# Decode attention over a long K/V cache: late MLP weights, eight stream buffers instead of six, and V before K on the tensor engine

## The chip, the cores and the metric

The kernel runs on one core of a Trainium2 chip. Times are device microseconds of one execution. The profiler's span, from the first to the last instruction, is 1.8 us shorter than the reported time (before: 702.1 of 703.9 us). Step times below are on the span's clock.

Engine names: PE is the tensor engine (PEld its weight loads), DVE the vector engine, ACT the scalar engine, POOL and SP the two others. SP issues nearly all loads.

## The reference, cut to what matters

One token passes through one block: layer norm, attention of 32 query heads over 8 K/V heads with 65,536 cached positions of 128 values each, output projection, residual, layer norm, a gated MLP with 1,792 hidden values, residual. All tensors are bf16.

```python
h  = x + (softmax(q @ k.T * Dh**-0.5) @ v) @ wo          # q = layernorm(x) @ wq
h2 = h + (sigmoid(hn @ w_gate) * (hn @ w_up)) @ w_down    # hn = layernorm(h)
```

K and V are 268 MB, the weights 14 MB; everything is read once, so the kernel is a stream of 282 MB through the core.

## The kernel before

K and V arrive as 128 tiles of 2 MB (128 partitions, 64 positions of 128 values in each). A K tile is transposed on PE, copied from PSUM by DVE and ACT, and multiplied with q ("S2"). A V tile is multiplied with the exponentials ("PV"). K of head h is interleaved with V of head h-1. SP issues the load of tile `ti` when tile `ti - NB` has been used up. The gate, up and down weights (5.5 MB) ride between early tiles. Cuts are marked.

```python
NB = 6
kvbuf = [sb(f"kvbuf{i}", [P, NSL, DH], BF) for i in range(NB)]
wg_sb = sb("wg_sb", [P, DC, F], BF); wu_sb = ...; wd_sb = ...
pexp = [sb(f"pexp{i}", [P, REP, CH], BF) for i in range(2)]
# ... wchunks: four pieces of wo on s_wo, then gate, up and two halves of down on s_wglu ...

def process_k_tile(h, t, b, vt, kti):
    pe.wait(s_buf[b], 16 * fill_count[b])
    # ... 64 transposes, evacuations, S2 groups three behind ...
    if vt is not None:
        pv_emit_all(vt)              # the V tile that came before this K tile

for ti, (kind, h, t) in enumerate(tiles):
    run_deferred(ti)
    b = ti % NB
    if ti - NB >= 0:
        sp.wait(ch_tile.sem, rel[ti - NB])
    # ... the last tile as four loads s_last[0..3] ...
    sp.dma(lambda e: e.dma_start(kvbuf[b][:, :, :], src_t), s_buf[b])
    wi = ti - (NB - 1)
    if 0 <= wi < len(wchunks):       # one weight piece after each of tiles 5 to 12
        sp.dma(wchunks[wi] ...)
    # ... process the tile ...

# the tail, after the last PV: softmax sum, o, output projection, layer norm, then
pe.wait(s_wglu, 16 * N_WGLU_DMA)
# ... 112 gate and up matmuls in two halves, tanh, product, 2 x 28 down matmuls, output ...
```

Of the kernel before, what the change touches and what calls it, by code (L numbers as in the profile page):

```python
# [5 lines left out]
BF = mybir.dt.bfloat16  # L6
F32 = mybir.dt.float32
ACTF = mybir.ActivationFunctionType
ALU = mybir.AluOpType
# [90 lines left out]
def bass_sequential_preLN__gqa_block_cached__glu_gated_glu__decode_kernel(  # L100
# [28 lines left out]
    FILL = min(128, CH)  # L129
    assert CH % FILL == 0 and FILL % GS == 0  # L130
    FPH = CH // FILL
    NB = 6
    NS = 5
    LAG = 3
    SCALE = float(DH) ** -0.5
# [24 lines left out]
    with ExitStack() as es:  # L160
# [6 lines left out]
        wbig = sb("wbig", [P, WBIG], BF)  # L167
        wq_v = wbig[:, 0:DC * HQ * DH].rearrange("p (c n) -> p c n", c=DC)
        wo_v = wbig[:, 0:HQ * D].rearrange("p (hd n) -> p hd n", hd=HQ)
        wg_sb = sb("wg_sb", [P, DC, F], BF)  # L170
        wu_sb = sb("wu_sb", [P, DC, F], BF)
        wd_sb = sb("wd_sb", [P, FC, D], BF)
        sc = [sb(f"sc{i}", [P, REP, CH], F32) for i in range(2)]
        pexp = [sb(f"pexp{i}", [P, REP, CH], BF) for i in range(2)]
        ident_f = sb("ident_f", [P, P], F32)
        ident_b = sb("ident_b", [P, P], BF)
        ones_f = sb("ones_f", [P, P], F32)
        onesD_f = sb("onesD_f", [P, P], F32)
        eps_t = sb("eps_t", [P, 1], F32)
        xcol_b = sb("xcol_b", [P, DC], BF)  # L180
        xx = sb("xx", [P, 2 * DC], F32)
        hh = sb("hh", [P, 2 * DC], F32)
        stat = sb("stat", [P, 8], F32)
# [10 lines left out]
        rs4 = sb("rs4", [P, 1], F32)  # L194
        o4_b = sb("o4_b", [P, P], BF)
        o_b = sb("o_b", [P, HQ], BF)
        attn_acc = sb("attn_acc", [P, DC], F32)
        th = sb("th", [P, FC], F32)
        sig = sb("sig", [P, FC], F32)
        hid_b = sb("hid_b", [P, FC], BF)  # L200
# [20 lines left out]
        s_wbig = sem("s_wbig")  # L221
        s_wo = sem("s_wo")
        s_x = sem("s_x")
        s_wglu = sem("s_wglu")
        s_out = sem("s_out")
        NQ_LAST = 4
        s_last = [sem(f"s_last{i}") for i in range(NQ_LAST)]
# [19 lines left out]
        def W(stream, inc):  # L247
# [17 lines left out]
            ),  # L265
            g_ident,
        )
        for c in range(DC):
            act.dma(
                lambda e, c=c: e.dma_start(  # L270
                    xcol_b[:, c:c + 1],
                    A_x[0, 0, c * P:(c + 1) * P].rearrange("(p o) -> p o", o=1),
                ),
                s_x,
            )

        def issue_wglu(stream):
# [11 lines left out]
            )  # L289

        sp.dma(
            lambda e: e.dma_start(wq_v, A_wq.rearrange("(c p) n -> p c n", p=P)),
            s_wbig,
        )

# [6 lines left out]
        W(dve, g_ident)  # L302
        d_identb = ch_dm.nxt()
        dve.ins(lambda e: e.tensor_copy(ident_b[:, :], ident_f[:, :]), d_identb)
        dve.wait(s_x, 16 * DC)
        d1 = ch_dm.nxt()
        dve.ins(lambda e: e.tensor_copy(xx[:, 0:DC], xcol_b[:, :]), d1)  # L307
        W(dve, d1)
        d_xx = ch_dm.nxt()
        dve.ins(lambda e: e.tensor_tensor(xx[:, DC:2 * DC], xx[:, 0:DC], xx[:, 0:DC], ALU.mult), d_xx)  # L310
# [81 lines left out]
        for q in range(4):  # L392
# [3 lines left out]
                    A_wo[q * HQ4 * P:(q + 1) * HQ4 * P, :].rearrange("(hd p) n -> p hd n", p=P),  # L396
                ), s_wo)
            )
        wchunks.append((False, lambda e: e.dma_start(wg_sb[:, :, :], B_w_gate.rearrange("(c p) f -> p c f", p=P)), s_wglu))
        wchunks.append((False, lambda e: e.dma_start(wu_sb[:, :, :], B_w_up.rearrange("(c p) f -> p c f", p=P)), s_wglu))  # L400
        FC2 = FC // 2
        wchunks.append((False, lambda e: e.dma_start(wd_sb[:, 0:FC2, :], B_w_down[0:FC2 * P, :].rearrange("(c p) d -> p c d", p=P)), s_wglu))
        wchunks.append((False, lambda e: e.dma_start(wd_sb[:, FC2:FC, :], B_w_down[FC2 * P:FC * P, :].rearrange("(c p) d -> p c d", p=P)), s_wglu))
        N_WO_DMA = 4
        N_WGLU_DMA = 4
        wo_issued[0] = True

        fill_count = {}
# [124 lines left out]
        def pe_bc(h):  # L533
            if sm_stage.get(h, 0) >= 2:
                return
            pe_tps(h)
            sm_stage[h] = 2
            hp = h % 2
            W(pe, diag_rec[h])
            W(pe, mb_last_read[0])  # L540
            inc = ch_pem.nxt()
            pe.ins(
                lambda e: e.matmul(  # L543
                    MB[:, MB_BC:MB_BC + REP], lhsT=ones_f[0:REP, :], rhs=diag[0:REP, 0:REP], start=True, stop=True
                ),
                inc,
            )
            bc_rec[h] = inc
            W(dve, inc)
            if (h - 2) in exp_rec:  # L550
                W(dve, exp_rec[h - 2])
            a1 = ch_dm.nxt()
            dve.ins(
                lambda e, hp=hp: e.tensor_scalar(  # L554
                    negmax[hp][:, :], MB[:, MB_BC:MB_BC + REP], -SCALE, None, op0=ALU.mult
                ),
                a1,
            )
            mb_last_read[0] = a1
            W(act, a1)  # L560
            if (h - 2) in pv_rec:
                W(act, pv_rec[h - 2])
            if (h - 2) in sum_rec:
                W(act, sum_rec[h - 2])
            last_inc = None
            for j in range(REP):
                inc_j = ch_am.nxt()
                act.ins(
                    lambda e, j=j, hp=hp: e.activation(  # L569
                        pexp[hp][:, j, :],  # L570
                        sc[hp][:, j, :],
                        ACTF.Exp,
                        bias=negmax[hp][:, j:j + 1],
                        scale=SCALE,
                        accum_out=rowsum[hp][:, j:j + 1],
                    ),
                    inc_j,
                )
                last_inc = inc_j
            exp_rec[h] = last_inc  # L580
            act_skip_until[0] = Gctr[0] + 6
# [42 lines left out]
        def pe_attn(h):  # L624
            if h in att_rec:
                return
            assert wo_issued[0]
            W(pe, o_ready[h])
            W(pe, mb_last_read[0])
            if h == 0:  # L630
                pe.wait(s_wo, 16 * N_WO_DMA)
            inc = None
            for c in range(DC):
                for j in range(REP):
                    hd = REP * h + j
                    last = (c == DC - 1 and j == REP - 1)
                    inc = ch_pem.nxt() if last else None
                    pe.ins(
                        lambda e, c=c, hd=hd, j=j: e.matmul(  # L639
                            MB[:, MB_ATT + c:MB_ATT + c + 1],  # L640
                            lhsT=wo_v[:, hd, c * P:(c + 1) * P],
                            rhs=o_b[:, hd:hd + 1],
                            start=(j == 0),
                            stop=(j == REP - 1),
                        ),
                        inc,
                    )
            att_rec[h] = inc
            W(dve, inc)
            if (h - 1) in attacc_rec:  # L650
                W(dve, attacc_rec[h - 1])
            a1 = ch_dm.nxt()
            if h == 0:
                dve.ins(lambda e: e.tensor_copy(attn_acc[:, :], MB[:, MB_ATT:MB_ATT + DC]), a1)
            else:
                dve.ins(
                    lambda e: e.tensor_tensor(
                        attn_acc[:, :], attn_acc[:, :], MB[:, MB_ATT:MB_ATT + DC], ALU.add
                    ),
                    a1,  # L660
                )
            attacc_rec[h] = a1
            mb_last_read[0] = a1
# [14 lines left out]
        def pv_emit_one(vt):  # L678
# [32 lines left out]
            vt.next_i = i + 1  # L711
            if i == NSL - 1 and t == TILES_PER_HEAD - 1:
                pe_sum_and_o(h)
                deferred.append((cur_ti[0] + 2, lambda h=h: pe_attn(h)))
            return True

        def pv_emit_all(vt):
# [64 lines left out]
        def run_deferred(ti):  # L782
            ready = [(thr, fn) for thr, fn in deferred if thr <= ti]
            deferred[:] = [(thr, fn) for thr, fn in deferred if thr > ti]
            for thr, fn in ready:
                fn()

        stash = []
        cur_ti = [0]
        rel = {}  # L790

        def process_k_tile(h, t, b, vt, kti):
            pe.wait(s_buf[b], 16 * fill_count[b])
            for gi in range(GPT):
                g = Gctr[0]
# [28 lines left out]
                if len(pendS2) > LAG:  # L824
                    sg = make_s2(pendS2.pop(0))
                    while s2_emit_one(sg):
                        pass
            if vt is not None:
                pv_emit_all(vt)

        for ti, (kind, h, t) in enumerate(tiles):
            cur_ti[0] = ti
# [26 lines left out]
            if kind == "K":  # L859
                vt = stash.pop(0) if stash else None  # L860
                process_k_tile(h, t, b, vt, ti)
                if t == TILES_PER_HEAD - 1:
                    deferred.append((ti + 2, lambda h=h: pe_tps(h)))
                    deferred.append((ti + 3, lambda h=h: pe_bc(h)))
            else:
                vt = make_vtile(h, t, b, ti)
                if ti + 1 < NT and tiles[ti + 1][0] == "K" and not stash:
# [10 lines left out]
            pe_attn(h)  # L878
        assert len(att_rec) == HKV

        W(dve, attacc_rec[HKV - 1])
        e1 = ch_dm.nxt()
        dve.ins(lambda e: e.tensor_tensor(hh[:, 0:DC], xx[:, 0:DC], attn_acc[:, :], ALU.add), e1)
        W(dve, e1)
        e2 = ch_dm.nxt()
        dve.ins(lambda e: e.tensor_tensor(hh[:, DC:2 * DC], hh[:, 0:DC], hh[:, 0:DC], ALU.mult), e2)
        W(pe, e2)
        W(pe, mb_last_read[0])
        p_st2 = ch_pem.nxt()
# [5 lines left out]
        )  # L895
        d_hn = ln_chain(stat2, hh[:, 0:DC], hn_b[:, :], p_st2)
        W(pe, d_hn)
        pe.wait(s_wglu, 16 * N_WGLU_DMA)
        FCH = (FC + 1) // 2
        halves = [(0, FCH), (FCH, FC)]  # L900
        gu_rec = []
# [49 lines left out]
        y_rec = []  # L951
        for hi, (f0, f1) in enumerate(halves):
            W(pe, hid_rec[hi])
            inc_y = None
            for c in range(DC):
                for fc in range(f0, f1):
# [16 lines left out]
        p_y = y_rec[-1]  # L973
        W(dve, y_rec[0])
        e5a = ch_dm.nxt()
        dve.ins(lambda e: e.tensor_tensor(hh[:, DC:2 * DC], hh[:, 0:DC], MB[:, MB_Y:MB_Y + DC], ALU.add), e5a)
        W(dve, e5a)
        W(dve, p_y)
        e5 = ch_dm.nxt()
# [68 lines left out]
```

## Time and profile before

| | before |
|---|---|
| reported time, median | 703.69 us (703.24 to 704.51, 13 runs) |
| span of the profiled run | 702.1 us |
| PE busy | 614.2 us, 87% |
| bytes read | 282.33 MB |
| last V bytes land (last of 16 engines) | 688.1 us |
| last PV matmul ends | 690.7 us |

The first fence is from the page of the kernel before: the DMA's busy share (in tenths) and its rate in 40 slices of 17.6 us, and two DMA queues with packets, bytes and the share of sixteen engines' time.

```profile
DMA  8999999999999999999999999899999999999980
GB/s 331 427 403 393 412 404 427 425 428 423 425 426 423 425 402 428 380 427 426 428 420 427 424 427 413 363 414 427 423 421 400 427 426 426 426 425 426 425 370 14
...
q1 hardware_dynamic: 26440, 282.34, 96.2%
q8 instruction: 100, 1.64, 0.9%
```

The load queue, q1, is busy 96.2% of the time of sixteen engines. The rate is 420 to 428 GB/s with a few dips and falls to 14 GB/s in the last slice: the tail runs with the DMA silent. Queue q8 the page calls "instruction": 100 packets, 1.64 MB, that no load of the kernel issues. I take them for fetches of instructions; e7 and e9 below add instructions, and the packets of such a queue grow with them.

The windows view of the kernel before, stretches of 6 us (the header names the columns):

```profile
core 0: us, PE busy (x) PEld busy (x) DVE busy (x) ACT busy (x) POOL busy (x), PEclk, DMA share, GB/s
282.00:288.00 6.00, 5.48 (x127) 5.22 (x124) 3.90 (x7) 2.79 (x3) 0.00 (x0) 1.00 0.82 303
444.00:450.00 6.00, 5.93 (x129) 5.57 (x125) 3.39 (x6) 2.05 (x2) 0.00 (x0) 1.00 0.81 298
672.00:678.00 6.00, 3.53 (x64) 3.34 (x60) 0.00 (x0) 0.00 (x0) 0.00 (x0) 1.00 0.99 412
678.00:684.00 6.00, 5.77 (x75) 5.78 (x76) 0.00 (x0) 0.00 (x0) 0.00 (x0) 0.72 0.71 293
684.00:690.00 6.00, 6.00 (x111) 6.00 (x109) 0.00 (x0) 0.00 (x0) 0.00 (x0) 1.00 0.14 54
690.00:696.00 6.00, 2.95 (x78) 2.62 (x75) 2.03 (x10) 1.58 (x2) 0.00 (x0) 0.98 0.01 3
```

There are two kinds of low rate. The stretches at 282 and 444 us are dips inside the stream. From 678 us on the stream runs out, and does so slowly: the DMA share is still 0.71 up to 684 us and 0.14 up to 690.

PE's waits for loads (total us, times, longest):

```profile
engine line waited for: us in total, times, longest us
PE TB L811 <- DMA kvbuf<-in_A_k_cache_dram: 28.5, 15, 9.7
...
PE OB L702 <- DMA kvbuf<-in_A_v_cache_dram: 4.7, 3, 2.7
```

The chain of waits at the end of the kernel before (start us, us, what):

```profile
653.81 24.37 DMA kvbuf<-in_A_v_cache_dram
...
678.23 12.51 PE OB L702 x192
...
691.84 0.57 PE MB L639 x16
...
694.93 3.07 PE SB L914 x112
698.00 0.86 PE MB L963 x28
698.86 0.76 PE OB L963 x28
```

The V load that PE waits for lands at 678.2 us, PE multiplies three V tiles in a row until 690.7, and output projection, layer norm and MLP follow up to 702.1.

What the views do not print is that one load completes sixteen times: the trace has each increment of a load's semaphore, and each of the 127 whole K and V tiles, and each quarter of the last, has sixteen. For the last quarter of the last V tile (us):

```
680.6 680.6 680.9 681.0 681.1 681.6 681.9 682.1 | 685.3 685.5 685.7 685.7 685.8 685.9 686.3 688.1
```

Eight completions are there by 682.1 and the other eight come 3 to 6 us after that. I read each as one of the sixteen DMA engines of the page having done its part, and "engine" stands for this reading below; the trace names no engine. The kernel waits for all sixteen (`16 * fill_count[b]`), so a wait for the load is a wait for the sixteenth.

### The profile page before, as it was taken

To read this page: it belongs to the slowest core of one execution; us is meant where nothing else is said; L and a number is where in the kernel's file an instruction comes from. 1 tells how busy PE (TensorE), PEld (TensorE's weight loads), DVE (VectorE), ACT (ScalarE), POOL (GpSimd) and SP (SyncE) were. 2 spreads that over 40 slices of the span, in tenths; PEclk is the share of its full clock that TensorE was granted. 3 is DMA by queue.
4 is the path that set the end of the run, shared out by engine and by line. 5 is a ranking of instruction groups with operands and counts; after the bars stand their busy time and mean duration, and the time that the engine had idled before them with its cause. 6 is when DMAs were issued, how large, how long until landed. Compare 5 with 4: busy or idle time off the path is not lost.

```text
span 702.1 us, 26598 instructions
## 1 busy us (share of the span) xinstructions
PE 614.2 (87%) x12773; PEld 596.8 (85%) x12773; DVE 307.3 (44%) x527; ACT 186.0 (26%) x225; POOL 0.7 (0%) x6
## 2 busy tenths in 40 slices
PE   0888838988999979999999988899899999999976
PEld 0887838988888979999988978899899998989876
DVE  0476634444644346443554336443454536343001
ACT  0343412221422124322323114221333223231201
POOL 0000000000000000000000000000000000000000
PEclk9999978999999989999999989999989999999998
DMA  8999999999999999999999999899999999999980
GB/s 331 427 403 393 412 404 427 425 428 423 425 426 423 425 402 428 380 427 426 428 420 427 424 427 413 363 414 427 423 421 400 427 426 426 426 425 426 425 370 14
DMA packets 27123, 284.04 MB, mean 405 GB/s; under 512 B 2824, under 2 KB 8712, under 8 KB 10248
## 3 DMA queue, kind: packets, MB, share of 16 engines
q1 hardware_dynamic: 26440, 282.34, 96.2%
q8 instruction: 100, 1.64, 0.9%
q10 hardware_dynamic: 576, 0.00, 0.0%
q14 instruction: 7, 0.06, 0.0%
HBM read 282.33 MB, written 0.00 MB: 402 GB/s over the span
## 4 chain that ended last, share of the span: by engine, by line
PE 56%; DMA 35%; DVE 5%; issue 3%; SPq 0%; ACTq 0%; ACT 0%; DVEq 0%
DMA kvbuf<-in_A_k_cache_dram 29%; PE TB L811 25%; PE OB L702 19%; PE SB L758 9%; DMA kvbuf<-in_A_v_cache_dram 3%; DMA xcol_b<-in_A_x_dram 2%; DVE kts L455 2%; DVE sc L489 1%; DVE cmtmp L470 1%; PE MB L374 1%; PE MB L639 0%; PE SB L914 0%; SPq L850 0%; DVE o_b L604 0%; DVE cm L468 0%
## 5 line engine op out<-in xcount | busy, mean ns | idle before, releaser
L811 PE MATMUL TB<-ident_b,kvbuf 128*128 128x128 bf16 x4096 | 324.1, 224 | 37.8 <-DMA kvbuf<-in_A_k_cache_dram 28.5
L455 DVE COPY kts<-TB 128x1024 bf16<-128x1024 bf16 x359 | 236.3, 688 | 230.0 <-PE TB L811 229.4
L811 PEld LDWEIGHTS TB<-ident_b,kvbuf 128*128 128x128 bf16 x4096 | 244.4, 100 | 45.9 <-DMA kvbuf<-in_A_k_cache_dram 30.5
L452 ACT ACTIVATE kts<-TB 128x1024 bf16<-128x1024 bf16 x153 | 156.5, 1023 | 365.8 <-PE TB L811 365.8
L702 PE MATMUL OB<-kvbuf,pexp 128*4 128x128 bf16 x4096 | 241.7, 220 | 7.4 <-DMA kvbuf<-in_A_v_cache_dram 4.7
L702 PEld LDWEIGHTS OB<-kvbuf,pexp 128*4 128x4 bf16 x4096 | 229.9, 87 | 10.4 <-DMA kvbuf<-in_A_v_cache_dram 5.3
L758 PE MATMUL SB<-qT_b,kts 128*128 128x4 bf16 x4096 | 176.3, 165 | 13.0 <-DVE kts L455 6.6
L758 PEld LDWEIGHTS SB<-qT_b,kts 128*128 128x128 bf16 x4096 | 156.8, 97 | 16.8 <-DVE kts L455 9.9
L489 DVE COPY sc<-SB 128x512 f32<-128x512 f32 x32 | 33.5, 1046 | 31.2 <-PE SB L758 30.7
L569 ACT ACTIVATE pexp<-sc,negmax 128x512 bf16<-128x512 f32 x32 | 22.7, 710 | 86.8 <-DVE negmax L554 86.8
L597 DVE RECIPROCAL rs<-MB 4x1 f32<-4x1 f32 x8 | 1.2, 156 | 54.8 <-PE MB L588 54.8
L470 DVE TENSOR_REDUCE cmtmp<-sc 128x4 f32<-128x512 f32 x24 | 16.5, 686 | 0.8
L315 PE MATMUL MB<-xx,onesD_f 128*128 128x8 f32 x2 | 0.6, 370 | 18.0 <-DVE xx L310 18.0
L315 PEld LDWEIGHTS MB<-xx,onesD_f 128*128 128x128 f32 x2 | 0.5, 309 | 18.0 <-DVE xx L310 18.0
L344 ACT ACTIVATE stat<-stat,eps_t 128x1 f32<-128x1 f32 x2 | 0.6, 294 | 54.2 <-DVE stat L336 54.2
L554 DVE TENSOR_SCALAR negmax<-MB 128x4 f32<-128x4 f32 x8 | 1.3, 160 | 23.9 <-PE MB L543 23.9
L517 DVE TENSOR_REDUCE gmax<-MB 4x1 f32<-4x128 f32 x8 | 2.2, 279 | 14.6 <-PE MB L506 14.6
L307 DVE CAST xx<-xcol_b 128x4 f32<-128x4 bf16 x1 | 0.2, 170 | 15.8 <-DMA xcol_b<-in_A_x_dram 15.8
L569 ACT ACTIVATION_READ_ACCUMULATOR pexp<-sc,negmax 128x1 f32 x32 | 6.0, 187 | 0.0
L612 PE MATMUL MB<-ident_b,o_b 4*128 4x4 bf16 x8 | 1.4, 173 | 5.1 <-DVE o_b L604 5.1
L468 DVE TENSOR_REDUCE cm<-sc 128x4 f32<-128x512 f32 x8 | 5.5, 686 | 0.7
L612 PEld LDWEIGHTS MB<-ident_b,o_b 4*128 4x128 bf16 x8 | 0.7, 90 | 5.9 <-DVE o_b L604 5.9
(56 smaller groups left out, 64.3 us busy)
## 6 DMA issues: line engine op xcount, KB each, us to landing
kvbuf<-in_A_k_cache_dram SPq DMA_DIRECT2D x64, 2048.0 KB, 19.1
kvbuf<-in_A_v_cache_dram SPq DMA_DIRECT2D x63, 2048.0 KB, 16.0
wbig<-in_A_wq_dram SPq DMA_DIRECT2D x1, 4096.0 KB, 14.3
wbig<-in_A_wo_dram SPq DMA_DIRECT2D x4, 1024.0 KB, 20.3
kvbuf<-in_A_v_cache_dram SPq DMA_DIRECT2D x4, 512.0 KB, 23.1
wg_sb<-in_B_w_gate_dram SPq DMA_DIRECT2D x1, 1792.0 KB, 20.3
wu_sb<-in_B_w_up_dram SPq DMA_DIRECT2D x1, 1792.0 KB, 25.7
wd_sb<-in_B_w_down_dram SPq DMA_DIRECT2D x2, 896.0 KB, 21.4
```

The source lines that it names most:

```text
L374: lambda e, j=j, c=c: e.matmul(MB[:, MB_Q + j:MB_Q + j + 1], lhsT=wq_v[:, c, j * DH:(j + 1) * DH], rhs=xn_b[:, c:c + 1], start=(c == 0), s ...
L452: stream.ins(lambda e, slot=slot, src=src: e.activation(slot[:, :], src, ACTF.Copy), inc)
L455: stream.ins(lambda e, slot=slot, src=src: e.tensor_copy(slot[:, :], src), inc)
L468: dve.ins(lambda e, hp=hp, src=src: e.tensor_reduce(cm[hp][:, :], src, AX.X, ALU.max), inc)
L470: dve.ins(lambda e, src=src: e.tensor_reduce(cmtmp[:, :], src, AX.X, ALU.max), inc)
L489: dve.ins(lambda e, dst=dst, src=src: e.tensor_copy(dst, src), inc)
L517: lambda e: e.tensor_reduce(gmax4[0:REP, :], MB[0:REP, MB_TPS:MB_TPS + P], AX.X, ALU.max), a1
L569: lambda e, j=j, hp=hp: e.activation(pexp[hp][:, j, :], sc[hp][:, j, :], ACTF.Exp, bias=negmax[hp][:, j:j + 1], scale=SCALE, accum_out=row ...
L612: lambda e: e.matmul(MB[:, MB_OT:MB_OT + REP], lhsT=o4_b[0:REP, :], rhs=ident_b[0:REP, 0:REP], start=True, stop=True),
L702: lambda e, b=b, i=i, c=c, hp=hp: e.matmul(OB[0:REP, 0:P], lhsT=pexp[hp][:, :, c], rhs=kvbuf[b][:, i, :], start=(c == 0), stop=(c == CH - ...
L758: lambda e, fb=fb, col=col, slot=slot, s_=s_, h=h: e.matmul(SB[:, fb, col:col + REP], lhsT=KTs[slot][:, s_ * P:(s_ + 1) * P], rhs=qT_b[:, ...
L811: lambda e, g=g, b=b, sl=sl, s_=s_: e.matmul(TB[:, g % 4, s_ * P:(s_ + 1) * P], lhsT=kvbuf[b][:, sl, :], rhs=ident_b[:, :], start=True, st ...
```

## The change

Its intent: let the 5.5 MB of MLP weights come after the last V bytes, under the tail that ran with the DMA silent, and keep more loads in flight. The gate and up weights then lie over the used part of the output weights, which, with a single pexp buffer, frees room for two more K/V buffers. The V tile's products come before the K tile's transposes. x, wq, gate and up are read in a layout where row 4p + c goes to partition p, which makes each partition's piece contiguous (wq 32 KB instead of 8 KB, gate and up 14 KB instead of 3.5 KB); for this x is loaded in both layouts and the output projection is done in both. The diff, cut to its core:

```diff
-    NB = 6
+    NB = 8
-        wg_sb = sb("wg_sb", [P, DC, F], BF)
-        wu_sb = sb("wu_sb", [P, DC, F], BF)
+        wg_sb = wbig[:, 0:DC * F].rearrange("p (c f) -> p c f", c=DC)
+        wu_sb = wbig[:, DC * F:2 * DC * F].rearrange("p (c f) -> p c f", c=DC)
-        pexp = [sb(f"pexp{i}", [P, REP, CH], BF) for i in range(2)]
+        pexp_single = sb("pexp", [P, REP, CH], BF)
+        pexp = [pexp_single, pexp_single]
+        act.dma(lambda e: e.dma_start(xcolA_b[:, :], A_x[0, 0, :].rearrange("(p c) -> p c", c=DC)), s_xA)
-            lambda e: e.dma_start(wq_v, A_wq.rearrange("(c p) n -> p c n", p=P)),
+            lambda e: e.dma_start(wq_v, A_wq.rearrange("(p c) n -> p c n", c=DC)),
-        wchunks.append((False, ... wg_sb ... s_wglu))     # and wu_sb, two halves of wd_sb
-        N_WGLU_DMA = 4
...  # exp(h) now waits for PV(h-1) instead of PV(h-2); bc(h), which spreads head h's maximum over the partitions, is put off until that is scheduled
+            for lay in (0, 1):      # output projection in both layouts, 32 matmuls a head
         def process_k_tile(h, t, b, vt, kti):
+            if vt is not None:
+                pv_emit_all(vt)
             pe.wait(s_buf[b], 16 * fill_count[b])
...
-            if vt is not None:
-                pv_emit_all(vt)
...  # after the loop over the tiles
+        W(sp, attacc_rec[HKV - 2])
+        sp.dma(lambda e: e.dma_start(wg_sb, B_w_gate.rearrange("(p c) f -> p c f", c=DC)), s_wgu)
+        sp.dma(lambda e: e.dma_start(wu_sb, B_w_up.rearrange("(p c) f -> p c f", c=DC)), s_wgu)
+        sp.dma(lambda e: e.dma_start(wd_sb[:, 0:FC2, :], ...), s_wd0)
+        sp.dma(lambda e: e.dma_start(wd_sb[:, FC2:FC, :], ...), s_wglu)
...
-        pe.wait(s_wglu, 16 * N_WGLU_DMA)
+        pe.wait(s_wgu, 32)
...
             W(pe, hid_rec[hi])
+            pe.wait(s_wd0 if hi == 0 else s_wglu, 16)
```

More of the change, by code (lines that the diff above doesn't have):

```diff
@@ L169, in bass_sequential_preLN__gqa_block_cached__glu_gated_glu__decode_kernel @@
         wo_v = wbig[:, 0:HQ * D].rearrange("p (hd n) -> p hd n", hd=HQ)
-        wg_sb = sb("wg_sb", [P, DC, F], BF)
-        wu_sb = sb("wu_sb", [P, DC, F], BF)
+        assert 2 * DC * F <= (HQ - REP) * D
+        wg_sb = wbig[:, 0:DC * F].rearrange("p (c f) -> p c f", c=DC)
+        wu_sb = wbig[:, DC * F:2 * DC * F].rearrange("p (c f) -> p c f", c=DC)
         wd_sb = sb("wd_sb", [P, FC, D], BF)
         sc = [sb(f"sc{i}", [P, REP, CH], F32) for i in range(2)]
-        pexp = [sb(f"pexp{i}", [P, REP, CH], BF) for i in range(2)]
+        pexp_single = sb("pexp", [P, REP, CH], BF)
+        pexp = [pexp_single, pexp_single]
         ident_f = sb("ident_f", [P, P], F32)
@@ L180, in bass_sequential_preLN__gqa_block_cached__glu_gated_glu__decode_kernel @@
         xcol_b = sb("xcol_b", [P, DC], BF)
+        xcolA_b = sb("xcolA_b", [P, DC], BF)
         xx = sb("xx", [P, 2 * DC], F32)
@@ L196, in bass_sequential_preLN__gqa_block_cached__glu_gated_glu__decode_kernel @@
         o_b = sb("o_b", [P, HQ], BF)
-        attn_acc = sb("attn_acc", [P, DC], F32)
+        attn_acc = sb("attn_acc", [P, 2 * DC], F32)
+        hstd = sb("hstd", [P, DC], F32)
         th = sb("th", [P, FC], F32)
@@ L223, in bass_sequential_preLN__gqa_block_cached__glu_gated_glu__decode_kernel @@
         s_x = sem("s_x")
+        s_xA = sem("s_xA")
         s_wglu = sem("s_wglu")
+        s_wgu = sem("s_wgu")
+        s_wd0 = sem("s_wd0")
         s_out = sem("s_out")
@@ L304, in bass_sequential_preLN__gqa_block_cached__glu_gated_glu__decode_kernel @@
         dve.ins(lambda e: e.tensor_copy(ident_b[:, :], ident_f[:, :]), d_identb)
-        dve.wait(s_x, 16 * DC)
+        dve.wait(s_xA, 16)
         d1 = ch_dm.nxt()
-        dve.ins(lambda e: e.tensor_copy(xx[:, 0:DC], xcol_b[:, :]), d1)
+        dve.ins(lambda e: e.tensor_copy(xx[:, 0:DC], xcolA_b[:, :]), d1)
         W(dve, d1)
@@ L398, in bass_sequential_preLN__gqa_block_cached__glu_gated_glu__decode_kernel @@
             )
-        wchunks.append((False, lambda e: e.dma_start(wg_sb[:, :, :], B_w_gate.rearrange("(c p) f -> p c f", p=P)), s_wglu))
-        wchunks.append((False, lambda e: e.dma_start(wu_sb[:, :, :], B_w_up.rearrange("(c p) f -> p c f", p=P)), s_wglu))
         FC2 = FC // 2
-        wchunks.append((False, lambda e: e.dma_start(wd_sb[:, 0:FC2, :], B_w_down[0:FC2 * P, :].rearrange("(c p) d -> p c d", p=P)), s_wglu))
-        wchunks.append((False, lambda e: e.dma_start(wd_sb[:, FC2:FC, :], B_w_down[FC2 * P:FC * P, :].rearrange("(c p) d -> p c d", p=P)), s_wglu))
         N_WO_DMA = 4
-        N_WGLU_DMA = 4
+        N_WGLU_DMA = 2
         wo_issued[0] = True
@@ L560, in pe_bc @@
             W(act, a1)
-            if (h - 2) in pv_rec:
-                W(act, pv_rec[h - 2])
+            if (h - 1) in pv_rec:
+                W(act, pv_rec[h - 1])
+            elif h >= 1:
+                raise AssertionError("PV of previous head must be scheduled before exp")
             if (h - 2) in sum_rec:
@@ L632, in pe_attn @@
             inc = None
-            for c in range(DC):
-                for j in range(REP):
-                    hd = REP * h + j
-                    last = (c == DC - 1 and j == REP - 1)
-                    inc = ch_pem.nxt() if last else None
-                    pe.ins(
-                        lambda e, c=c, hd=hd, j=j: e.matmul(
-                            MB[:, MB_ATT + c:MB_ATT + c + 1],
-                            lhsT=wo_v[:, hd, c * P:(c + 1) * P],
-                            rhs=o_b[:, hd:hd + 1],
-                            start=(j == 0),
-                            stop=(j == REP - 1),
-                        ),
-                        inc,
-                    )
+            for lay in (0, 1):
+                for c in range(DC):
+                    cols = wo_v[:, :, c::DC] if lay == 0 else wo_v[:, :, c * P:(c + 1) * P]
+                    for j in range(REP):
+                        hd = REP * h + j
+                        last = (lay == 1 and c == DC - 1 and j == REP - 1)
+                        inc = ch_pem.nxt() if last else None
+                        pe.ins(
+                            lambda e, c=c, hd=hd, j=j, lay=lay, cols=cols: e.matmul(
+                                MB[:, MB_ATT + lay * DC + c:MB_ATT + lay * DC + c + 1],
+                                lhsT=cols[:, hd, :],
+                                rhs=o_b[:, hd:hd + 1],
+                                start=(j == 0),
+                                stop=(j == REP - 1),
+                            ),
+                            inc,
+                        )
             att_rec[h] = inc
@@ L653, in pe_attn @@
             if h == 0:
-                dve.ins(lambda e: e.tensor_copy(attn_acc[:, :], MB[:, MB_ATT:MB_ATT + DC]), a1)
+                dve.ins(lambda e: e.tensor_copy(attn_acc[:, :], MB[:, MB_ATT:MB_ATT + 2 * DC]), a1)
             else:
@@ L657, in pe_attn @@
                     lambda e: e.tensor_tensor(
-                        attn_acc[:, :], attn_acc[:, :], MB[:, MB_ATT:MB_ATT + DC], ALU.add
+                        attn_acc[:, :], attn_acc[:, :], MB[:, MB_ATT:MB_ATT + 2 * DC], ALU.add
                     ),
@@ L713, in pv_emit_one @@
                 pe_sum_and_o(h)
-                deferred.append((cur_ti[0] + 2, lambda h=h: pe_attn(h)))
+                deferred.append((cur_ti[0] + 1, lambda h=h: pe_attn(h)))
             return True
@@ L785, in run_deferred, with bc_when_ready @@
             for thr, fn in ready:
-                fn()
+                if fn() is False:
+                    deferred.append((thr + 1, fn))
+        def bc_when_ready(h):
+            if h >= 1 and (h - 1) not in pv_rec:
+                return False
+            pe_bc(h)
+            return True
         stash = []
@@ L863, in bass_sequential_preLN__gqa_block_cached__glu_gated_glu__decode_kernel @@
                     deferred.append((ti + 2, lambda h=h: pe_tps(h)))
-                    deferred.append((ti + 3, lambda h=h: pe_bc(h)))
+                    deferred.append((ti + 3, lambda h=h: bc_when_ready(h)))
             else:
@@ L879, in bass_sequential_preLN__gqa_block_cached__glu_gated_glu__decode_kernel @@
         assert len(att_rec) == HKV
+        W(sp, attacc_rec[HKV - 2])
+        sp.dma(lambda e: e.dma_start(wg_sb, B_w_gate.rearrange("(p c) f -> p c f", c=DC)), s_wgu)
+        sp.dma(lambda e: e.dma_start(wu_sb, B_w_up.rearrange("(p c) f -> p c f", c=DC)), s_wgu)
+        sp.dma(lambda e: e.dma_start(wd_sb[:, 0:FC2, :], B_w_down[0:FC2 * P, :].rearrange("(c p) d -> p c d", p=P)), s_wd0)
+        sp.dma(lambda e: e.dma_start(wd_sb[:, FC2:FC, :], B_w_down[FC2 * P:FC * P, :].rearrange("(c p) d -> p c d", p=P)), s_wglu)
         W(dve, attacc_rec[HKV - 1])
         e1 = ch_dm.nxt()
-        dve.ins(lambda e: e.tensor_tensor(hh[:, 0:DC], xx[:, 0:DC], attn_acc[:, :], ALU.add), e1)
+        dve.ins(lambda e: e.tensor_tensor(hh[:, 0:DC], xx[:, 0:DC], attn_acc[:, 0:DC], ALU.add), e1)
         W(dve, e1)
@@ L886, in bass_sequential_preLN__gqa_block_cached__glu_gated_glu__decode_kernel @@
         dve.ins(lambda e: e.tensor_tensor(hh[:, DC:2 * DC], hh[:, 0:DC], hh[:, 0:DC], ALU.mult), e2)
+        dve.wait(s_x, 16 * DC)
+        W(dve, e2)
+        e_hs0 = ch_dm.nxt()
+        dve.ins(lambda e: e.tensor_copy(hstd[:, :], xcol_b[:, :]), e_hs0)
+        W(dve, e_hs0)
+        e_hs = ch_dm.nxt()
+        dve.ins(lambda e: e.tensor_tensor(hstd[:, :], hstd[:, :], attn_acc[:, DC:2 * DC], ALU.add), e_hs)
         W(pe, e2)
@@ L975, in bass_sequential_preLN__gqa_block_cached__glu_gated_glu__decode_kernel @@
         e5a = ch_dm.nxt()
-        dve.ins(lambda e: e.tensor_tensor(hh[:, DC:2 * DC], hh[:, 0:DC], MB[:, MB_Y:MB_Y + DC], ALU.add), e5a)
+        W(dve, e_hs)
+        dve.ins(lambda e: e.tensor_tensor(hh[:, DC:2 * DC], hstd[:, :], MB[:, MB_Y:MB_Y + DC], ALU.add), e5a)
         W(dve, e5a)
```

## The prediction

> **What bounds it now.** DMA. The page's queue table has the load queue at 96.2% of sixteen engines over the 702.1 us span. PE is busy 87%, but the waits view gives PE 33 us idle for loads of K and V, and where nothing is late a K tile takes PE 5.15 us and a V tile 3.74 us (8.9 us a pair), against two 2 MB loads at about 5.06 us each.
>
> [...] in the completion records of one tile load the first and the sixteenth are up to 8 us apart. From tile 13 to 41 the first completions step by 4.89 us a tile, the last by 5.06. The slow engines never run dry (their next tile is always issued before they finish one); the dips in the windows view (258 to 264, 282 to 288, 438 to 450 us: 298 to 374 GB/s) are fast engines waiting for buffers. I estimate the slow ones are those that also carry the 100 instruction-fetch packets of 16 KB (queue 8, mean 1.06 us). The last engine finishes V at 688.1 us; then PE has 2.6 us of PV left, and the output projection, LN and GLU run to 702.1 with DMA silent.
>
> **What the change does.**
> 1. Gate, up and down weights (5.5 MB; 14.8 us, estimated from 26 GB/s an engine, and 327 GB/s measured for 1 KB packets) move behind the last V load. Loads after tile 13 land about 14 us earlier; the stream carries the same bytes, so its end hardly moves. Gate/up pieces grow from 3.5 KB to 14 KB: 398 to about 423 GB/s, 0.5 us.
> 2. Eight buffers instead of six: removes dips of fast engines (about 7 us of their time). Worth almost nothing, since the slow engines set the end.
> 3. Earlier x (one small load) and V before K on PE: PE starts 2 to 4 us earlier and waits more evenly; off the critical path.
> 4. Costs: 128 more output-projection matmuls (16 take 0.55 us; hidden), 2 small DVE operations. With one pexp buffer the last exp (4 x 0.71 us and its chain) no longer hides under a PV: PE stops about 4 us near the last head, then catches up 1.3 us in each V tile that follows.
>
> **The new end** (span): the stream ends at 687 us with the down weights' second half. Last V chunk about 672.5, PV done 673.5, normalized h 678, gate/up weights 681.5, gate/up done 684.5, then the wait for the last down weights, then 3.4 us (last 28 matmuls to the end, as before: 698.7 to 702.1). Span 690.5, reported time 1.9 us more: **692.3 us**, 1.7% faster. Range 688 to 697. Faster by over 2%: 0.22; within 2%: 0.76; slower: 0.02.
>
> **Checks in the profile.** The chain of waits ends with the down matmuls' wait for their weights, near 687. Last V completion 670 to 675. First-to-sixteenth spread of a tile grows beyond 8 us, the last-engine step stays 5.0 to 5.1 us. Dips of the DMA share between 250 and 540 us mostly vanish. PE starts at 16 to 18 us instead of 20.
>
> **What would make it wrong.** If slow engines do gain from deeper buffers (step down to 4.95), the time falls to about 680. If PE becomes the limit (more half-clock stretches, the single pexp buffer stalling each head), the last PV ends after 680 and the time stays near 697 or more.

Where its numbers come from: in the trace of the kernel before, 16 KB packets took 620 ns at the mean (26.4 GB/s for one engine, 423 for sixteen), packets of 3.5 KB 144.2 ns (398 GB/s for sixteen) and of 1 KB 50.2 ns (326), and the 100 packets of q8 have 16,384 bytes and took 1.06 us. The rates are estimates from these durations. The completions of one tile are up to 8.6 us apart, and each tile's load was issued 4.4 us or more before the last completion of the tile before it. The granted clock was 0.5 in nine stretches of 3.4 to 10.2 us. That the dips are fast engines waiting for buffers was the author's estimate. The sum: the stream's end at 687, then 3.4 us, put at 690.5, and 1.9 us more, put at 692.3.

## The result, and the profile after

The changed kernel takes 691.08 us (690.87 to 691.38, 8 runs) against 703.69 us. The ratio is 0.9821, 95% interval 0.9811 to 0.983. Ratios here and below are the mean time of one kernel's fast runs over that of the other's of the same rounds, so not quite the ratio of the medians. The span is 689.3 us.

The same rows of the page after (slices of 17.2 us):

```profile
DMA  8999999999999999999999999999999999999974
GB/s 337 424 428 396 400 428 423 424 424 426 426 423 424 424 428 424 425 424 425 425 423 426 425 425 425 425 425 425 425 424 426 425 424 424 427 426 422 424 312 169
...
q1 hardware_dynamic: 25288, 282.34, 97.4%
q8 instruction: 101, 1.65, 1.0%
```

The dips between 200 and 600 us are gone. The last two slices are no longer 370 and 14 GB/s but 312 and 169: the DMA now works under the tail. The bytes are the same. Instruction fetches number 101.

The windows that answer to those before, with the columns as there:

```profile
282.00:288.00 6.00, 6.00 (x127) 5.88 (x124) 1.92 (x3) 1.33 (x2) 0.00 (x0) 1.00 1.02 429
444.00:450.00 6.00, 6.00 (x131) 5.89 (x129) 2.16 (x3) 1.89 (x2) 0.00 (x0) 1.00 0.99 418
660.00:666.00 6.00, 4.84 (x85) 4.52 (x82) 0.00 (x0) 0.00 (x0) 0.00 (x0) 1.00 0.78 308
672.00:678.00 6.00, 4.32 (x85) 3.96 (x81) 1.57 (x9) 0.00 (x0) 0.00 (x0) 1.00 0.73 284
678.00:684.00 6.00, 3.10 (x116) 3.10 (x117) 1.14 (x6) 1.75 (x3) 0.00 (x0) 0.52 0.50 184
```

At 282 and 444 us the DMA share is full. At 660 us it is already below 0.8 (0.78): engines are idle again, though weights are still to come. PE's waits for loads:

```profile
PE OB L710 <- DMA kvbuf<-in_A_v_cache_dram: 9.6, 9, 2.1
...
PE TB L828 <- DMA kvbuf<-in_A_k_cache_dram: 3.8, 7, 1.5
PE SB L942 <- DMA wbig<-in_B_w_up_dram: 3.0, 1, 3.0
```

PE waited 33.2 us for K and V before and waits 13.4 us now, plus 3.0 us for the gate and up weights. The chain of waits at the end:

```profile
639.06 41.80 DMA wbig<-in_B_w_up_dram
...
680.90 3.14 PE SB L942 x112
684.05 0.24 PE MB L992 x9
684.29 1.09 issue
685.38 0.67 PE MB L992 x19
686.05 0.76 PE OB L992 x28
```

The gate and up matmuls (L942) start when the last of their weights land at 680.9 us, and the second half of down (L992 into OB) follows the first at 685.9, with its weights there since 685.6.

The sixteen completions of the last quarter of the last V tile in the changed kernel:

```
652.1 652.2 652.2 652.2 652.5 653.1 653.8 656.4 | 670.6 670.6 670.7 670.7 670.8 671.0 672.1 672.3
```

Eight engines have done their part at 656.4 us at the latest. The other eight need until 672.3. The sixteenth completion of a tile moved along by 5.05 us a tile before and by 5.04 us after (tiles 24 to 126). That of the first engine went from 5.03 to 4.89 us. Two more buffers let the punctual engines run ahead, and the late ones keep their pace.

### The profile page after: what moved, and what is told of

It is laid out like the page before. It is cut to its first block, busy times and chain, and to the rows that moved or that the text cites. A ratio compares the mean times of both kernels' runs of the same rounds, so it can differ in the third digit from the quotient of the medians.

```text
span 689.3 us, 26864 instructions
## 1 busy us (share of the span) xinstructions
PE 617.6 (90%) x12901; PEld 598.4 (87%) x12901; DVE 308.5 (45%) x529; ACT 185.8 (27%) x225; POOL 0.7 (0%) x6
## 3 DMA queue, kind: packets, MB, share of 16 engines
q1 hardware_dynamic: 25288, 282.34, 97.4%
q8 instruction: 101, 1.65, 1.0%
## 4 chain that ended last, share of the span: by engine, by line
PE 53%; DMA 38%; DVE 5%; issue 3%; ACT 0%; SPq 0%; DVEq 0%
PE TB L828 26%; DMA kvbuf<-in_A_k_cache_dram 20%; PE OB L710 15%; DMA kvbuf<-in_A_v_cache_dram 10%; PE SB L766 9%; DMA wbig<-in_B_w_up_dram 6%; DVE kts L459 2%; DMA xcolA_b<-in_A_x_dram 2%; DVE sc L493 1%; PE MB L647 1%; PE MB L382 1%; DVE cmtmp L474 1%; DVE cm L472 0%; PE SB L942 0%; ACT kts L456 0%
## 5 line engine op out<-in xcount | busy, mean ns | idle before, releaser
L828 PE MATMUL TB<-ident_b,kvbuf 128*128 128x128 bf16 x4096 | 316.8, 221 | 15.9 <-issue 9.8
L828 PEld LDWEIGHTS TB<-ident_b,kvbuf 128*128 128x128 bf16 x4096 | 238.6, 98 | 23.2 <-issue 13.2
L710 PE MATMUL OB<-kvbuf,pexp 128*4 128x128 bf16 x4096 | 245.4, 221 | 14.1 <-DMA kvbuf<-in_A_v_cache_dram 9.6
L710 PEld LDWEIGHTS OB<-kvbuf,pexp 128*4 128x4 bf16 x4096 | 233.2, 88 | 18.9 <-DMA kvbuf<-in_A_v_cache_dram 11.2
L323 PE MATMUL MB<-xx,onesD_f 128*128 128x8 f32 x2 | 0.6, 372 | 13.7 <-DVE xx L318 13.7
L323 PEld LDWEIGHTS MB<-xx,onesD_f 128*128 128x128 f32 x2 | 0.5, 312 | 13.7 <-DVE xx L318 13.7
L647 PE MATMUL MB<-o_b,wbig 128*128 128x1 bf16 x256 | 8.7, 168 | 2.6 <-DVE negmax L558 2.3
L647 PEld LDWEIGHTS MB<-o_b,wbig 128*128 128x128 bf16 x256 | 8.1, 107 | 3.2 <-DVE negmax L558 2.4
L942 PE MATMUL SB<-hn_b,wbig 128*128 128x1 bf16 x112 | 3.1, 165 | 3.0 <-DMA wbig<-in_B_w_up_dram 3.0
## 6 DMA issues: line engine op xcount, KB each, us to landing
wbig<-in_A_wo_dram SPq DMA_DIRECT2D x4, 1024.0 KB, 17.2
wbig<-in_B_w_gate_dram SPq DMA_DIRECT2D x1, 1792.0 KB, 26.4
```

What stands on the lines that cost most here:

```text
L647: lambda e, c=c, hd=hd, j=j, lay=lay, cols=cols: e.matmul(MB[:, MB_ATT + lay * DC + c:MB_ATT + lay * DC + c + 1], lhsT=cols[:, hd, :], rhs ...
L710: lambda e, b=b, i=i, c=c, hp=hp: e.matmul(OB[0:REP, 0:P], lhsT=pexp[hp][:, :, c], rhs=kvbuf[b][:, i, :], start=(c == 0), stop=(c == CH - ...
L828: lambda e, g=g, b=b, sl=sl, s_=s_: e.matmul(TB[:, g % 4, s_ * P:(s_ + 1) * P], lhsT=kvbuf[b][:, sl, :], rhs=ident_b[:, :], start=True, st ...
L942: lambda e, col=col, wsb=wsb, fc=fc, c=c, bank=bank: e.matmul(SB[:, bank, col:col + 1], lhsT=wsb[:, c, fc * P:(fc + 1) * P], rhs=hn_b[:, c ...
```

## The experiments

Theory: **the eight late engines' share of the byte stream sets the end.** Then the change gains by what it takes from behind the last V byte, and nothing by smoothing the stream, by PE's order or by an earlier start. Rivals: the deeper buffers gain (the dips are gone); PE's order gains (PE waits 20 us less). Each of the twelve runs gave correct output. The median of the kernel before was 703.34 to 703.47 us in these runs (one of its runs beside e1, e2 and e3 took 706.16 us, which widens their intervals).

| run | time, us | ratio to before (95% interval) |
|---|---|---|
| the change | 691.08 | 0.9821 (0.9811 to 0.983) |
| e1 late weights alone | 692.59 | 0.9843 (0.9822 to 0.9864) |
| e2 the change with six buffers | 691.29 | 0.9824 (0.9799 to 0.9848) |
| e3 the rest without late weights, six buffers | 702.32 | 0.9982 (0.9961 to 1.0003) |
| e4 probe of the engines | 692.23 | one run |
| e5 quarter tiles cut at partition 125 | 713.94 | 1.0151 (1.0136 to 1.0167) |
| e6 its control | 708.43 | 1.0082 (1.0061 to 1.0102) |
| e7 3,073 idle instructions on POOL | 691.25 | 0.9827 (0.9813 to 0.9842) |
| e8 late weights, one wait | 696.06 | 0.9897 (0.9882 to 0.9911) |
| e9 6,145 idle instructions on POOL | 704.60 | 1.0019 (1.0004 to 1.0034) |
| e10 down weights in 7 KB pieces | 693.91 | 0.9868 (0.9853 to 0.9883) |
| e11 the change again | 691.21 | 0.9830 (0.9815 to 0.9844) |
| e12 the change, K before V | 691.31 | 0.9831 (0.9814 to 0.9847) |

### Which part of the change gains: e1, e2, e3, e12

e1 is the kernel before with the weight loads moved:

```diff
-        wchunks.append((False, ... wg_sb ..., s_wglu))   # and wu_sb, wd_sb twice
+        # after the loop over the tiles, layouts unchanged
+        sp.dma(... wg_sb ..., s_wgu); sp.dma(... wu_sb ..., s_wgu)
+        sp.dma(... wd_sb[:, 0:FC2, :] ..., s_wd0); sp.dma(... wd_sb[:, FC2:FC, :] ..., s_wglu)
-        pe.wait(s_wglu, 16 * N_WGLU_DMA)
+        pe.wait(s_wgu, 32)                                # and s_wd0, s_wglu before the down halves
```

> The old kernel (six buffers, two pexp, K before V) with one thing changed: the gate, up and down weights are loaded after the last V load, each under its own wait. Slow-engine theory (the byte stream of the eight late DMA engines sets the end, so only what lies behind the last V counts): nearly the whole gain, 691.5 to 693.5 us, as 3.5 KB weight pieces cost about 0.5 us more than the change's 14 KB ones. Rival, deeper buffers (the gain is the vanished dips of the DMA rate): under half of the gain, 698 us or more. Rival, PE order and earlier start: 696 us or more.

e2 is the change with one line undone, `NB = 6`:

> The changed kernel with six K/V buffers instead of eight. Slow-engine theory: same as the changed kernel within 1.5 us (690 to 692.5), although the dips of the DMA rate return. Deeper-buffers rival: 696 us or more.

e3 is the change with the weights early again, in buffers of their own, and so with six K/V buffers:

> Everything of the change but the late weights and the two buffers they make room for: gate, up and down weights load early into buffers of their own, six K/V buffers; V before K, single pexp, early x, (p c) layouts stay. Slow-engine theory: like the old kernel, 702.5 to 704.5 us. Rival, PE order and earlier start: 698 us or less.

e12 is the change with `pv_emit_all(vt)` back behind the K tile:

> The changed kernel with the old order on PE: the K tile's transposes first, the waiting V tile's products after. Slow-engine theory: PE has slack, so the same as the changed kernel within 1 us (690.2 to 692.2). Rival, PE order: 695 us or more.

Measured: 692.59, 691.29, 702.32 and 691.31 us. Moving the weights alone gains 10.8 us (703.36 to 692.59). All the rest without it gains 1.0 us, a little more than e3 was expected to (702.5 us at the least), and its interval still includes no gain. Taking the two buffers out of the changed kernel costs 0.2 us (691.29 against 691.08), and putting the old order back costs 0.1 us (691.31 against 691.21), both within the runs' scatter. Both rivals fall: neither the two buffers nor the order is worth 0.3 us in the changed kernel, and e1 does without both and keeps 10.8 us of the gain. In e1 the chain of waits ends as the theory has it, at the down weights:

```profile
670.65 17.09 DMA wd_sb<-in_B_w_down_dram
...
687.78 0.92 PE OB L967 x28
```

The 1.3 us between e1 and e2 come from what else the change does, contiguous pieces and the earlier x among it; they were not taken apart further. In e1 the last V bytes land at 673.8 us and in e2 at 672.8; the weights take 13.9 us more in e1 and 13.3 us in e2.

### One wait or three: e8

e8 is e1 with all four weight loads on one semaphore, waited for before the first gate matmul, as in the kernel before.

> The old kernel with the gate, up and down weights behind the last V load as in e1_move_only, but under a single wait for all four loads before the first gate matmul, as the old kernel has it. The end is the last landing, then gate and up (3.1 us) and the first half of down (about 1 us) that no longer hide under it: 3 to 4.5 us more than e1_move_only, 695.5 to 697 us.

Measured: 696.06 us, 3.5 us more than e1. The chain shows the gate, up and first down matmuls that e1 hides, now behind the landing:

```profile
670.29 16.78 DMA wd_sb<-in_B_w_down_dram
...
687.11 3.14 PE SB L915 x112
690.25 0.75 PE MB L964 x28
691.00 0.84 PE OB L964 x28
```

So the three waits are a third of the gain that the move makes: the late loads gain 7.4 us under one wait and 10.8 us if each is waited for where it is used.

### Which engines are late: e4

The author's assumption was that a load of k rows runs on k engines, the same ones for every load of k rows, and that one row more adds one engine to them. On that assumption a load of k rows queues behind what its k engines have to do, which makes it an instrument.

```diff
+            if ti == 100:
+                for k_ in range(1, 17):
+                    sp.dma(lambda e, k_=k_: e.dma_start(probe[0:k_, k_ - 1, :], A_k_cache[0, 0, 0:k_, 0:8]),
+                           s_probe[k_ - 1])
```

> The changed kernel, with sixteen tiny loads queued behind tile 100; the one numbered k has k rows[...]. Their completions tell which engines lag. Instruction-fetch theory: eight engines lag by about 15 us and they form a fixed set[...]. If the lag were random among engines, the count of late completions would not be a steady function of k. Time within 1.5 us of the changed kernel.

The completions of the probes, from the trace's semaphore records. Each probe below 16 rows also has one early record at its issue, left out here. Punctual completions fell at 520 to 527 us, late ones at 534 to 538:

```
rows      1  2  3  4  5  6  7  8  9 10 11 12 13 14 15 16
punctual  1  2  3  4  5  5  5  6  7  7  7  7  7  7  7  8
late      0  0  0  0  0  1  2  2  2  3  4  5  6  7  8  8
```

The k-row probe has k completions, as assumed. The row counts that add a late one are 6, 7 and 10 to 15. The late ones come 13 to 17 us after the first, in every probe that has any, and neither count ever falls from one k to the next. That agrees with a fixed set of eight late engines and with sets that grow with k; which engines these are the trace does not show.

### Why they are late: e7 and e9

The trace suggests a cause, an estimate until e7 and e9. A K/V packet of 16 KB takes 613 ns at the median. In the changed kernel 111 of 16,256 took over 800 ns, and 100 of those overlap one of the 101 instruction-fetch packets of q8 (16 KB and 1.07 us each); of all 16,256 only 26% overlap one. The bytes fit PE's stream: its 25,802 matmuls and weight loads, at 64 bytes each, are the 1.65 MB of q8 (the runs below give 64 bytes: 24 packets of 8,192 for 3,073 instructions). To test it, fetches were added without any other work. POOL is idle (0.7 us busy), so it got waits on a semaphore that is already there:

```diff
+        for n_ in range(6144):           # e9: 12288
+            pool.ops.append(("wait", g_ident[0], g_ident[1]))
```

> The changed kernel, with 6,144 waits on a semaphore that is already there put into the idle POOL engine's stream: about 24 more instruction-fetch packets of 16 KB, no other work. Instruction-fetch theory: the engines that carry those packets get later, by about 24 x 1.3 us in total. If they are the same eight as for PE: about 4 us on each, and 694 to 696 us. If they are other engines, which have some 20 us to spare: no change of time, but those show later completions. If fetches do not cause the lag: no change in either.

> As e7_more_fetches, but 12,288 waits on the idle POOL engine, so some 48 extra fetch packets. In e7 the 24 made exactly one of the eight punctual engines 16 us later at the last V chunk, 0.69 us each, still ahead of the eight late ones, and the time did not move. Slow-engine theory: 48 make that engine about 33 us later than the punctual ones, 12 to 13 us behind the other late ones, so it alone now sets the end: 701 to 705 us. Rival (the end is set by the mean rate of all engines or by PE): the extra bytes are 0.4 MB, under 1 us, so 691 to 692.5 us.

The build packs two waits into one instruction, so e7 has 3,073 more instructions and e9 6,145 (29,937 and 33,009 on their pages, 26,864 in the changed kernel). With them come 24 and 48 more packets, of 8 KB (not of 16 KB, which was estimated from q8's). The page of e9, fetch queues alone:

```profile
q8 instruction: 101, 1.65, 1.0%
q14 instruction: 55, 0.45, 0.2%
```

Queue 14 had 7 packets in the changed kernel, 31 in e7, and has 55 here. The sixteen completions of the last quarter of V in the changed kernel, e7 and e9 (us):

```
change 652.1 652.2 652.2 652.2 652.5 653.1 653.8 656.4 670.6 670.6 670.7 670.7 670.8 671.0 672.1 672.3
e7     651.9 651.9 652.0 652.2 653.1 653.5 656.3 668.6 670.6 670.6 670.8 670.8 670.9 671.1 672.1 672.4
e9     661.6 661.7 661.8 661.8 662.0 662.1 663.5 670.9 670.9 671.0 671.0 671.1 671.2 671.7 672.8 686.1
```

In e7 exactly one punctual engine is now late, at 668.6 instead of 652 to 654. It is still earlier than the eight, and the time does not move (691.25 us). In e9 the fetches, doubled, put one engine at 686.1 us, 13.8 us behind the last one of the changed kernel (672.3). The eight late ones stay where they were. The remaining seven have moved to 661.6 to 663.5 us. The time is 704.60 us, 13.4 us more than the change: the whole gain is gone, through instructions that do nothing on an engine that has nothing to do. The timeline of e9 shows the end waiting for V, for gate and up, and for down in turn:

```profile
681.17 7.31 PE L712 MATMUL OB<-kvbuf,pexp 128*4 128x128 bf16 x128 [1.16 <-DMA kvbuf<-in_A_v_cache_dram]
...
694.73 3.15 PE L944 MATMUL SB<-hn_b,wbig 128*128 128x1 bf16 x112 [2.82 <-DMA wbig<-in_B_w_up_dram]
...
699.46 0.91 PE L994 MATMUL OB<-hid_b,wd_sb 128*128 128x1 bf16 x28 [0.83 <-DMA wd_sb<-in_B_w_down_dram]
```

This is the strongest test of the theory, as the two runs differ only in a count and one of them had to be without effect. It shows that added instructions, with the packets that fetch them, make a DMA engine late (one completion at 668.6 us with 24 more packets, at 686.1 with 48), and that the latest one sets the end (691.25 and 704.60 us). That PE's own fetches are what delays the eight was not tested by a run: PE's stream was not shortened. The trace of the changed kernel speaks for it by its times, though. Over the 106 steps from tile 20 to tile 126, the eight late completions together fall behind the punctual pace by 1.2 to 1.8 us in 81 steps and by less than 0.2 us in the other 25. Just 81 fetches of q8 fall into this stretch, at most one to a step, and if each step is counted from 0.7 us before the mean of the eight late completions (a shift chosen to fit), 104 of the 106 steps agree: a loss where there is a fetch, none where there is none. The loss of the eight late ones is 124 us in all, that of the eight punctual ones 4.6.

### A try to use it: e5 and e6

By the theory, the end would come earlier if the late engines carried less. In e4 no probe of up to five rows has a late completion. A load of 125 partitions leaves five completions (in the trace of e5 the two pieces of a cut, of 125 and 3 partitions, leave 10 completion records instead of 32: 5 and 3, and an early one for each). That these five are the punctual ones of the probes was not shown. e5 loads a quarter of five tiles in this way; e6 makes the same cut at 112, where both pieces leave sixteen completions (the DMA view of e6 gives their landings, 34.3 and 37.0 us after the issue for the K pieces, which it does only for loads with sixteen).

```diff
+            elif ti in (40, 62, 84, 106, 122):
+                Q3 = NSL * 3 // 4
+                for p0, p1, i0, i1 in ((0, P, 0, Q3), (0, 125, Q3, NSL), (125, P, Q3, NSL)):   # e6: 112
+                    sp.dma(... kvbuf[b][p0:p1, i0:i1, :], src_t[p0:p1, i0:i1, :] ..., s_buf[b])
```

> The changed kernel, where the last quarter (0.5 MB) of five K/V tiles (40, 62, 84, 106, 122) is loaded by two DMAs of 125 and 3 partitions instead of being part of one of 128. [...] Slow-engine theory: each late engine carries 5 x 33 KB less, at 26.8 GB/s 6.1 us; the end comes 5 to 6 us earlier, 685 to 686.5 us, with the first-to-sixteenth spread of the last tile near 14 us or less instead of 20. If the end is not set by the late engines (rival: total bytes over 16 engines, or PE): no gain, 690.5 us or more.

(The 6.1 us are an estimate from 16 KB packets of some 612 ns, 26.8 GB/s for one engine.)

> Control for the one before: the same five quarters cut off in the same way, but at partition 112, so that both pieces (112 and 16 partitions) run on sixteen engines. Same number of DMAs, no bytes moved between engines. Slow-engine theory: 690.5 to 692.5 us. If the cut itself helps, it shows here.

Measured: 713.94 and 708.43 us, both far off. The control alone costs 17.2 us against the change's 691.21, 3.4 us a cut, and e5 is 5.5 us slower than its control where the theory had it faster. In e6 the 4 KB packets of the cut quarters took 254 ns at the median, where those of the changed kernel's last V tile took 159 ns. That is under 1 us of a cut's 3.4 (8 such packets an engine); packets of 16 KB were long too, 464 of them over 800 ns instead of 111. In all, the load queue's packets took 97.3% of 706.2 us in e6 and 97.4% of 689.3 in the changed kernel, some 16 us more for the same bytes. Why the packets are longer no run here shows; the cause stays open. So these two do not test the theory, since the cut costs more than the 6 us that the shift could gain. Whether bytes can be moved off the late engines without that cost stays open.

### The other try: e10, with e11 beside it

e10 reads the down weights so that partition p holds rows 14p to 14p + 13, in 7 KB pieces instead of seven of 1 KB; the hidden values must then be produced in that order, so gate and up take every fourteenth column. e11 is the change itself.

```diff
-  B_w_down[0:FC2 * P, :].rearrange("(c p) d -> p c d", p=P)
+  B_w_down.rearrange("(p c) d -> p c d", c=FC)[:, 0:FC2, :]       # and the second half
-                                lhsT=wsb[:, c, fc * P:(fc + 1) * P],
+                                lhsT=wsb[:, c, fc::FC],
```

> The changed kernel with the down weights laid out so that each partition reads 7 KB in a row instead of seven pieces of 1 KB (row f = 14p + c; the gate and up matmuls pick the matching columns with a stride of 14). Slow-engine theory: 1.84 MB at about 420 instead of 327 GB/s, 1.2 us less for every engine at the very end: 689.5 to 690.5 us, against the changed kernel of the same rounds. If the end were PE's: no change.

> The changed kernel itself, on the same chip as the other three, for comparison: 690.5 to 691.7 us by every theory.

Measured: 693.91 us against 691.21: 2.7 us slower. The last down weights land at 685.4 us instead of 686.0 (e11), so the expected 1.2 us was 0.6, and only 0.2 against the first profile of the change (685.6). And the gate and up matmuls got slower. The timeline of the changed kernel, then of e10 (weight loads and matmuls):

```profile
680.90 3.06 PEld L942 LDWEIGHTS SB<-hn_b,wbig 128*128 128x128 bf16 x112 [3.12 <-DMA wbig<-in_B_w_up_dram]
680.90 3.14 PE L942 MATMUL SB<-hn_b,wbig 128*128 128x1 bf16 x112 [3.03 <-DMA wbig<-in_B_w_up_dram]
```

```profile
681.11 6.80 PEld L942 LDWEIGHTS SB<-hn_b,wbig 128*128 128x128 bf16 x112 [2.85 <-DMA wbig<-in_B_w_up_dram]
681.12 6.88 PE L942 MATMUL SB<-hn_b,wbig 128*128 128x1 bf16 x112 [2.76 <-DMA wbig<-in_B_w_up_dram]
```

With a stride of 14 values the 112 weight loads keep PEld busy 6.80 us instead of 3.06, and the end becomes PE's. The change's own strided loads (every fourth value, in the output projection) show no such cost: its 32 loads a head, half of them strided, keep PEld busy 1.01 us, where 16 plain ones before took 0.47. No version here beats the change.

## Why the prediction was right

| step | predicted, us | measured, us |
|---|---|---|
| last V bytes | 672.5 | 672.3 |
| last PV matmul ends | 673.5 | 674.4 |
| normalized h | 678 | 679.2 |
| gate and up weights there | 681.5 | 680.9 |
| gate and up done | 684.5 | 684.0 |
| last down weights | 687 | 685.6 |
| span | 690.5 | 689.3 |
| time | 692.3 | 691.08 |

- **The late engines set the pace: right.** The step of the sixteenth completion was predicted at 5.0 to 5.1 us and is 5.04; the spread of a tile was to grow beyond 8 us and reaches 20.3. It was 8.6 before, 8.8 in e1, and 17 with either the eight buffers or the new order alone (e12, e2): these let the punctual engines run ahead, to no use.
- **They are late from instruction fetches: right**, an estimate then. In e7 and e9 added fetches delay one engine, 24 packets by some 16 us, the next 24 by 17.5 (686.1 against 668.6), and the trace's times agree with PE's own fetches delaying the eight, by 1.5 us a fetch (124 us in 81 steps). The total time alone would not have told this from a stream at its mean rate: 5.5 MB at the page's 402 GB/s are 13.7 us too.
- **Eight buffers are worth almost nothing: right**, 0.2 us (e2), although the dips of the DMA rate vanish as predicted. I take the dips for idle time of the punctual engines: in the changed kernel the first completion of a tile comes up to 20.3 us before the sixteenth, before 8.6, and the sixteenth keeps its step of 5.04 us.
- **Order and early start are off the path: right** within 1.3 us. q's matmuls start at 15.8 us instead of 20.1. The contiguous pieces, put at 0.5 us, are part of these 1.3.
- **The stream's end was 1.4 us too late in the prediction.** The mis-sized term is the cost of the down weights' 1 KB pieces: I took 327 GB/s, from the mean duration of such packets in the early phase (50.2 ns), for 5.6 of 14.8 us. The four late loads take 13.3 us behind the last V, 4.7 of them for down: 112 packets an engine, 42 ns each, although their durations there are 48.1 ns at the mean (46 at the median), which would be 5.4 us for 112. In part, then, the durations overlap, and a rate taken from them is too low. e10 shows that larger pieces save only 0.6 us there.
- **The last link of the chain was off.** I named the wait for the down weights. In e1 it is there. In the changed kernel the chain runs over gate and up, then a stop of 1.09 us of PE inside the first down half, which the profile puts to "issue"; the down weights land 0.3 us before they are used. The two paths are nearly level. I take that stop for a wait for instructions, by its time: PE has 19 stops over 0.3 us that the profile puts to "issue"; 18 of them, this one too, end 1.2 to 1.6 us after a fetch packet of q8 has ended, though fetches are 6.7 us apart. They last 0.3 to 1.5 us, 13.8 us in all. The 19th is the one of the next point. So the fetches seem to slow PE as well, here by 1.09 us on the last path; no run tested it.
- **The single pexp buffer cost less than 4 us.** PE stops 1.92 us before the last head's first PV, which starts at 640.3 us, 0.2 us after the last exp has ended, and catches up as predicted: its V matmuls wait for loads again at 657 us.

The timeline of the changed kernel shows this stop, and the issues of the late loads. Three of these took SP 13.1, 5.2 and 15.5 us, and a K load at 25 us took it 25.8, against 0.3 us for most loads; what sets it was not tested:

```profile
639.06 13.10 SPq L898 DMA_DIRECT2D wbig<-in_B_w_up_dram  x1
...
640.33 16.08 PE L710 MATMUL OB<-kvbuf,pexp 128*4 128x128 bf16 x256 [1.92 <-issue]
652.20 5.18 SPq L899 DMA_DIRECT2D wd_sb<-in_B_w_down_dram  x1
...
657.41 3.74 PE L710 MATMUL OB<-kvbuf,pexp 128*4 128x128 bf16 x64 [0.99 <-DMA kvbuf<-in_A_v_cache_dram]
657.42 15.52 SPq L900 DMA_DIRECT2D wd_sb<-in_B_w_down_dram  x1
```

## What to carry to other kernels

In a kernel bound by its stream, look at what still runs when the stream is over: loads that are only needed there belong behind the last bytes of the stream, each under its own wait (10.8 us here, 7.4 with one wait). The kernel waits for all sixteen completions of a load, and here they came up to 20.3 us apart, so read the slowest completion before you credit a change that smooths the mean rate. And count instructions, also those of idle engines: 6,145 of them on POOL, with the 48 packets that fetched them, cost 13.4 us here, and 3,073 with 24 packets nothing.
